# Group 2's first matmul as seven products of half-groups, and token-stationary second matmuls in groups 0 and 1

## The chip, the core and the metric

The kernel runs on one core of a Trainium2 chip. The metric is the device time of one execution in microseconds. A run gives a time; one profiled execution gives a span, which begins at its first instruction, and all durations quoted here. A core has five engines with queues of their own, which run in order and wait for each other only by semaphores: TensorE (PE in the profile, with its weight loads as PEld), VectorE (DVE), ScalarE (ACT), GpSimd (POOL) and SyncE (SP). Data lie in on-chip memory with 128 partitions; matmuls write into eight PSUM banks of 512 floats per partition.

## What is computed

```
w = softmax(weight, axis=-1)                       # [8 heads, 7 taps]
y[b, s, h, :] = sum_k w[h, k] * x_pad[b, s + k, h, :]   # causal window, 24 channels a head
xn = (y - mean(y)) / sqrt(var(y) + 1e-6) * g_ln    # over 192 channels
out = y + relu(xn @ w_ch1) @ w_ch2                 # 192 -> 768 -> 192
```

x is 8 x 4224 x 192 in float32; w_ch1, w_ch2 and g_ln come as float64 and are turned into float32 on the chip. The mean is taken out of w_ch1 in advance ("centring"), and the factor 1/sqrt(var) of a token, `rstd`, is applied to the result of the second matmul, so the first matmul can run on y itself.

## The kernel before

Tokens are worked on in 18 groups. Group 0 has 6 tokens in each of 128 partitions, group 1 has 8 (the rows left over in all batches), group 2 has 10, and groups 3 to 17 have 16. For each group the steps are:

- `first_tap` (ScalarE, L380) writes `y = x * tap 0`, `second_tap` (ScalarE, L398) writes tap 1 into a tile `tb`, and `add_second_tap` (L409) adds `tb` to `y` by an accumulating DMA that GpSimd issues. `conv` (VectorE, L417) adds the other taps, one instruction per tap and head.
- `transpose` (VectorE, L428) makes `yt`, in which a partition block of 32 holds 32 channels. `moments` (VectorE, L448) and `root` (20 small GpSimd operations, L460 to L483) make `rstd`. `store_y` writes y to the output.
- The first matmul: `up` for groups 0 to 2, `up_mixed` for the others. `rows_of_tiles` (L533) is the matmul of both: 32 rows of weights, 128 columns, four at a time, one for each block of 32 partitions.
- The second matmul: `down` (L785) for groups 0 and 1, `down_fast` (L838) from group 2 on; its result is scaled and added to the output by DMA.

`up` runs six passes of 128 hidden columns. Each takes a set of four banks (`take_set`), and ScalarE evicts it with the relu (L523). `take_set` and `take_bank` hand out the eight banks in rotation.

`up_mixed` and `down_fast` replace 8 block products by 7. The operands are cut into quarters, a11 to a22 of y (halves of the tokens by halves of the channels) and b11 to b22 of the weights; sums of the quarters are made beforehand (`sums_of_y`, `w1sums`, `w2sums`; `b12` is replaced by `b12 - b11`). Two bank sets X and Y take the products by turns. A set is read out by ScalarE between products, and some quarters of the result are closed by adding a second product, by an accumulating DMA (`add_by_dma`, L612) or by VectorE (L651). Only after that can ScalarE apply the relu (L658). `lower_sum` and `half_sum` prepare the operands of the second matmul.

`down` of groups 0 and 1 holds 32 columns of w2 as weights and streams the hidden values, so its result is transposed: `park` copies it out of PSUM (ScalarE, L913), `finish` transposes it back (VectorE, L965), and `scale` (ScalarE, L927) applies `rstd`.

The order of the work is written out by hand: instructions run on each engine in the order in which the Python program emits them. The loop over groups at the end emits, for group 0 and 1, what the other engines do during their first matmul and then `down`; `between` puts ScalarE and GpSimd work between the six passes of `up`; `work` is a list of ScalarE pieces that `down_fast` emits behind each of its products, `behind` says how many. `let_in(tile)` is a VectorE write of one element, which makes a later GpSimd write to the tile wait until VectorE has come to that place. Tiles with the same tag share a buffer: y[4] takes the buffer of y[2], and so waits for its store.

The hidden values of all groups lie in one tile, `room` (L184), 12288 floats in each partition. `tb[3]` lies at its end.

Of the kernel before, what the change touches and what calls it, by code (L numbers as in the profile page):

```python
# [16 lines left out]
def kernel(  # L17
# [69 lines left out]
    FC = NF // 2  # L87

# [295 lines left out]
    def second_tap(g, heads=(0, H)):  # L384

        n = groups[g][2]
        if heads[0]:
            pass
        elif g == 2:
            part = upool.tile([P, 3 * HJ * CH * C], F32, tag="ys", name="tb2")  # L390
            tb[g] = part[:, 0 : n * D].rearrange("p (j d) -> p j d", d=D)
        elif g == 3:
            tb[g] = room[:, (NF * NQ * C - D) * J :].rearrange("p (j d) -> p j d", d=D)
        else:
            tb[g] = bpool.tile([P, J, D], F32, tag="tb", name=f"tb{g}")
# [97 lines left out]
    def hidden_tile(g):  # L493
        n = groups[g][2]

        if fast[g]:
            ht[g] = room.rearrange(
                "p (h e f q j t) -> p h e f q j t", h=2, e=2, f=FC, q=NQ, t=width(g)
            )
        else:  # L500
            ht[g] = room[:, 0 : NF * NQ * n * C].rearrange(
                "p (f q j t) -> p f q j t", f=NF, q=NQ, t=C
# [6 lines left out]
    def evict_up(g, f, src):  # L509

        if not fast[g]:
            dst = ht[g][:, f]
# [26 lines left out]
    def between(g, f):  # L539

        if g == 1 and f > 2:
            second_tap(3, heads=[(0, 2), (2, 5), (5, 6)][f - 3])
        elif g == 2:
            if f == 0:
                scale(0, 0, groups[0][2])
                add_to_out(0, 0, groups[0][2])
                nc.gpsimd.memset(xg[4][0:1, 0:PAD, :], 0.0)
            elif f < 3:
                m = groups[1][2]
                scale(1, m * (f - 1) // 2, m * f // 2)  # L550
# [38 lines left out]
    def quarters_of_y(g):  # L589
        if width(g) == C:  # L590
            cuts = [(slice(HJ * h, HJ * h + HJ), slice(0, C)) for h in range(2)]
        else:
            cuts = [(slice(0, J), slice(T * h, T * h + T)) for h in range(2)]
        return [yt[g][:, js, CH * k : CH * k + CH, ts] for js, ts in cuts for k in range(2)]

    def sums_of_y(g, engine):

        room = upool.tile([P, 3 * HJ * CH * C], F32, tag="ys", name=f"ysums{g}")
        room = room.rearrange("p (v j c t) -> p v j c t", v=3, c=CH, t=width(g))
# [11 lines left out]
    def add_by_dma(dst, src):  # L611
        nc.gpsimd.dma_start(out=dst, in_=src, accum_op=ALU.add)  # L612

# [158 lines left out]
    po = {}  # L772

    def down(g):


        n = groups[g][2]
        po[g] = []
        js = slice(0, n)
        w = n * C  # L780
        for c in range(NC):
            bank = take_bank()
            for f in range(NF):
                for q in range(NQ):
                    nc.tensor.matmul(  # L785
                        bank[C * q : C * q + C, 0:w], w2[:, f, C * c : C * c + C], ht[g][:, f, q],
                        start=(f == 0), stop=(f == NF - 1),
                    )
            po[g].append((c, js, bank[:, 0:w]))
# [19 lines left out]
    def lower_sum(g, fs=range(FC)):  # L809

        a = of_products(g)
        if g in MIXED:
# [8 lines left out]
    def down_fast(g, work):  # L821
# [32 lines left out]
        if g == 2:  # L854
            work += [lambda h=h: first_tap(4, heads=(h, h + 1)) for h in range(7, H)]
# [6 lines left out]
        behind = (1, 1, 1, 1) if g == 2 else (3, 2, 2, 3)  # L862
# [42 lines left out]

    def park(g):

        n = groups[g][2]
        pool, room = (cpool, NC * NFAST * C) if g else (bpool, J * D)
        parked = pool.tile([P, room], F32, tag="cs" if g else "tb", name=f"parked{g}")  # L910
        parked = parked[:, 0 : NC * n * C].rearrange("p (c t) -> p c t", c=NC)
        for i, (c, js, src) in enumerate(po[g]):
            nc.scalar.copy(parked[:, c, :], src)  # L913
            po[g][i] = (c, js, parked[:, c, :])
# [38 lines left out]

    def down_rows(g, j):

        rows = take_bank()[:, 0:D]
        for f in range(NF):
            left = rows_left[g][:, f, j - fast[g]]
            nc.tensor.matmul(rows, left, w2[:, f], start=(f == 0), stop=(f == NF - 1))  # L959
        return rows  # L960

    def finish(g):
        ot = out_tile(g)
        for c, js, src in po.pop(g):
            nc.vector.transpose(  # L965
                ot[:, js, C * c : C * c + C], src.rearrange("p (j t) -> p j t", t=C)
            )

# [51 lines left out]
    for g in range(NG):  # L1020
# [59 lines left out]
        if last:  # L1080
# [4 lines left out]
            for j in range(fast[g], groups[g][2]):  # L1085
                add(g, j, down_rows(g, j))
# [34 lines left out]
```

## Time and profile before

| | |
|---|---|
| three runs | 957.99, 958.59 (median), 960.07 us |
| the profiled execution | 958.71 us, span 956.6 us |
| TensorE clock granted | 0.999 |
| TensorE busy | 948.1 us |
| VectorE busy | 891.1 us |
| ScalarE busy | 699.5 us |
| GpSimd busy | 337.9 us |
| first matmul of group 0 / 1 / 2 starts at | 23.05 / 48.85 / 80.28 us |
| second matmul of group 2 starts at | 99.87 us |
| first matmul of group 3 starts at | 117.12 us |

The time is 2.1 us above the span of the same execution. In the lines of the profile, "L417 DVE SCALAR_TENSOR_TENSOR y<-xg,taps,y" is an instruction of kernel line 417 on VectorE that writes y from xg, taps and y; "x40" counts instructions; a line of a timeline begins with the start and the duration in us, and the brackets at its end give the idle time before it and what ended that. Matmuls are pipelined, so their durations overlap, and the pace is read from starts. Each float32 matmul is recorded as two instructions. A line can be that of a helper: L533 is every first matmul, L838 every second matmul by products.

### The profile page before, as it was taken

The numbers are of one execution on the slowest core, as the hardware profiler recorded it, in microseconds if no ns is written. First come the engines' busy times: TensorE is split into PE (matmuls) and PEld (weight loads), VectorE is DVE, ScalarE is ACT, GpSimd is POOL, SyncE is SP. The second block draws the span as 40 slices with busy tenths as digits, with TensorE's granted clock in tenths as the row PEclk, the third lists the DMA queues.
The fourth block names the chain that finished last, engine by engine and source line by source line (L and its number), as shares of the span: only waits on it lengthen the run. The fifth ranks groups of instructions, "written<-read, shape, count | busy, mean of one in ns | idle before, by whom it ended". The sixth has DMA issues, their size and how long they took to land.

```text
span 956.6 us, 38719 instructions
## 1 busy us (share of the span) xinstructions
PE 948.1 (99%) x17266; PEld 725.7 (76%) x17266; DVE 891.1 (93%) x1501; ACT 699.5 (73%) x1174; POOL 337.9 (35%) x472
## 2 busy tenths in 40 slices
PE   8999999999999999999999999999999999999998
PEld 7886886776869687686968778795877869586787
DVE  8989999989999999999999999999999999999757
ACT  7755678586877959687795968779696877967462
POOL 1157522623145142534217141452316332261310
PEclk9999999999999999999999999999999999999999
DMA  8359689589697888979698897969889697778251
GB/s 204 111 153 213 116 224 273 112 178 242 135 258 144 240 162 178 226 136 273 128 250 153 192 221 130 276 131 249 159 194 213 128 275 134 173 136 137 42 96 67
DMA packets 39547, 168.87 MB, mean 177 GB/s; under 512 B 4437, under 2 KB 8150, under 8 KB 33367
## 3 DMA queue, kind: packets, MB, share of 16 engines
q0 software_dynamic: 32576, 106.25, 59.9%
q1 hardware_dynamic: 6800, 60.16, 17.4%
q8 instruction: 135, 2.21, 0.9%
q14 instruction: 30, 0.25, 0.1%
q10 hardware_dynamic: 6, 0.00, 0.0%
HBM read 38.93 MB, written 50.33 MB: 93 GB/s over the span
## 4 chain that ended last, share of the span: by engine, by line
PE 94%; DMA 2%; POOL 1%; DVE 1%; ACT 1%; issue 0%; SPq 0%; ACTq 0%; DVEq 0%; POOLq 0%
PE ps L533 46%; PE ps L838 44%; PE ps L785 3%; DMA xg<-in_x_dram 1%; DVE y L417 1%; PE ps L959 1%; DMA room<-room 1%; DMA out_dram<-y 1%; ACT room L645 0%; ACT y L380 0%; POOL room L612 0%; POOL d L460 0%; POOL r L483 0%; POOL d L479 0%; POOL d L478 0%
## 5 line engine op out<-in xcount | busy, mean ns | idle before, releaser
L417 DVE SCALAR_TENSOR_TENSOR y<-xg,taps,y 128x384 f32<-128x384 f32 (+3 forms) x720 | 361.9, 580 | 3.9 <-DMA y<-tb 2.6
L838 PE MATMUL ps<-room,w2sums 128*32 128x256 f32 (+2 forms) x4608 | 247.4, 371 | 0.0
L533 PE MATMUL ps<-yt,w 32*128 32x256 f32 (+2 forms) x4104 | 235.3, 379 | 2.1 <-DVE yt L428 1.0
L645 ACT COPY room<-ps 128x1024 f32<-128x1024 f32 (+1 forms) x135 | 175.1, 1297 | 79.6 <-PE ps L533 78.6
L533 PEld LDWEIGHTS ps<-yt,w 32*128 32x128 f32 x4104 | 203.7, 185 | 28.9 <-issue 10.1
L838 PEld LDWEIGHTS ps<-room,w2sums 128*32 128x32 f32 x4608 | 149.7, 110 | 91.6 <-ACT room L658 5.3
L838 PE MATMUL ps<-room,w 128*32 128x256 f32 (+2 forms) x3456 | 189.3, 371 | 0.0
L805 DVE TENSOR_TENSOR room<-room 128x1024 f32<-128x1024 f32 (+2 forms) x147 | 161.2, 1171 | 20.8 <-PE ps L838 14.1
L838 PEld LDWEIGHTS ps<-room,w 128*32 128x32 f32 x3456 | 112.3, 110 | 68.9 <-DVE room L651 5.0
L533 PE MATMUL ps<-ysums,w1sums 32*128 32x256 f32 x2160 | 125.2, 379 | 0.0
L533 PEld LDWEIGHTS ps<-ysums,w1sums 32*128 32x128 f32 x2160 | 109.0, 185 | 11.0 <-ACT room L645 3.3
L938 POOL DMA_DIRECT2D out_dram<-ot x69 | 59.3, 989 | 162.1 <-ACT ot L927 105.3
L409 POOL DMA_DIRECT2D y<-tb x59 | 52.5, 1386 | 152.5 <-ACT room L844 110.4
L844 ACT COPY cs<-ps 128x256 f32<-128x256 f32 (+2 forms) x192 | 69.7, 365 | 45.1 <-PE ps L838 45.1
L927 ACT ACTIVATE ot<-ot,r 128x192 f32<-128x192 f32 x232 | 93.9, 462 | 0.0
L658 ACT ACTIVATE room<-room 128x1024 f32<-128x1024 f32 (+1 forms) x89 | 92.7, 1072 | 1.5 <-DMA room<-parts_cs 1.4
L380 ACT ACTIVATE y<-xg,taps 128x384 f32<-128x384 f32 (+3 forms) x141 | 73.2, 608 | 1.2 <-DMA xg<-in_x_dram 0.6
L448 DVE BATCH_NORM_STATS2 st<-y 128x6 f32<-128x192 f32 x264 | 70.1, 346 | 0.0
L844 ACT COPY room<-ps 128x256 f32<-128x256 f32 (+2 forms) x96 | 35.7, 372 | 46.1 <-PE ps L838 44.5
L398 ACT ACTIVATE tb<-xg,taps 128x384 f32<-128x384 f32 (+1 forms) x120 | 66.3, 632 | 0.0
L533 PE MATMUL ps<-yt,w1sums 32*128 32x256 f32 x1080 | 65.4, 381 | 0.4 <-ACT room L645 0.4
L533 PE MATMUL ps<-ysums,w 32*128 32x256 f32 x1080 | 64.5, 376 | 0.0
(113 smaller groups left out, 906.4 us busy)
## 6 DMA issues: line engine op xcount, KB each, us to landing
xg<-in_x_dram SPq DMA_DIRECT2D x14, 2112.0 KB, 16.4
room<-room POOLq DMA_DIRECT2D x45, 512.0 KB, 5.1
out_dram<-ot POOLq DMA_DIRECT2D x59, 384.0 KB, 9.6
y<-tb POOLq DMA_DIRECT2D x58, 384.0 KB, 8.4
out_dram<-y SPq DMA_DIRECT2D x13, 1536.0 KB, 9.5
room<-parts_cs POOLq DMA_DIRECT2D x28, 512.0 KB, 6.9
room<-parts_tb POOLq DMA_DIRECT2D x14, 1024.0 KB, 7.6
xg<-in_x_dram POOLq DMA_DIRECT2D x1, 2112.0 KB, 14.6
```

Source lines behind the costliest of these rows:

```text
L380: nc.scalar.mul(y[g][:, 0:n, cs], xg[g][:, 0:n, cs], taps[:, h, 0:1])
L398: nc.scalar.mul(tb[g][:, 0:n, cs], xg[g][:, 1 : 1 + n, cs], taps[:, h, 1:2])
L417: nc.vector.scalar_tensor_tensor(out=y[g][:, 0:n, cs], in0=t[:, k : k + n, cs], scalar=taps[:, h, k : k + 1], in1=y[g][:, 0:n, cs], op0=AL ...
L448: nc.vector.bn_stats(out=sums[g][:, j, :], in_=y[g][:, j, :])
L533: nc.tensor.matmul(banks[:, q, i * w : i * w + w], right[rows, c, P * i : P * i + P], left[rows, :, c, :], start=(first and c == 0 and i = ...
L645: nc.scalar.activation(dst, src, AF.Relu) if relu else nc.scalar.copy(dst, src)
L658: nc.scalar.activation(c, c, AF.Relu)
L805: nc.vector.tensor_tensor(a[:, *dst, f], a[:, *left, f], a[:, *right, f], op=op)
L838: nc.tensor.matmul(dst[C * q : C * q + C, 0:w], right[:, f, C * c : C * c + C], left[:, f, q], start=(first and f == PAIR), stop=(f == PAI ...
L844: nc.scalar.copy(to[:, c], dst[:, 0:w].rearrange("p (j t) -> p j t", t=t))
L927: nc.scalar.mul(ots[g][:, j, :], ots[g][:, j, :], rstd[g][:, j : j + 1])
L938: nc.gpsimd.dma_start(out=rows[:, d0:d1], in_=src[:, d0:d1], accum_op=ALU.add)
```

## The change

- Group 2's first matmul is made by a new function, `up_whole`: the seven products of `up_mixed` in one pass over all hidden columns, with half-groups of 5 tokens, so each matmul streams 5 x 32 = 160 columns and a set of banks holds 3 x 160 = 480 columns each. The quarter c11 is closed by DMA through a tile of the tag "cs", c22 by DMA through one of the tag "tb", c21 by VectorE. The relus follow.
- `down` of groups 0 and 1 holds 128 tokens of hidden values as weights and streams w2 (192 columns), one row of tokens after another. ScalarE evicts the rows: a copy for group 0, which is scaled later, a multiplication by `rstd` for group 1. `park` and `finish` are gone.
- The sums that group 2's products need are made earlier: the third of `w1sums` in group 0 (by VectorE instead of GpSimd), `b12 - b11`, `sums_of_y(2)` and `moments(2)` in group 1. GpSimd's first three `w2sums` come ahead of the addition of group 3's second tap, behind a `let_in`.
- ScalarE makes group 3's second tap for five heads instead of six; VectorE makes the sixth. The scaling and the output DMAs of groups 0 and 1 and the first taps of group 4 move.

The diff, cut to its core:

```diff
+    FROM_2 = 2 * FC * NQ * J * T - FC * NQ * (J - 6) * C
...
-            tb[g] = room[:, (NF * NQ * C - D) * J :].rearrange("p (j d) -> p j d", d=D)
+            tb[g] = room[:, NF * J * P - n * 5 * GRP :].rearrange("p (j d) -> p j d", d=5 * GRP)
...
     def between(g, f):
         if g == 1 and f > 2:
-            second_tap(3, heads=[(0, 2), (2, 5), (5, 6)][f - 3])
-        elif g == 2:
-            if f == 0:
-                scale(0, 0, groups[0][2])
-                add_to_out(0, 0, groups[0][2])
-                nc.gpsimd.memset(xg[4][0:1, 0:PAD, :], 0.0)
-            elif f < 3:
-                m = groups[1][2]
-                scale(1, m * (f - 1) // 2, m * f // 2)
-                if f == 2:
-                    add_to_out(1, 0, m)
-            else:
-                first_tap(4, heads=[(0, 3), (3, 6), (6, 7)][f - 3])
+            second_tap(3, heads=[(0, 2), (2, 4), (4, 5)][f - 3])
...
+    def up_whole(g):
...
+        X, Y = take_set(), take_set()
...
+        def close(c, banks, pool, tag):
+            part = pool.tile([P, J * D], F32, tag=tag, name=f"parts_{tag}{g}")
+            part = part[:, 0 : FC * NQ * w]
+            nc.scalar.copy(part.rearrange("p (f q w) -> p f q w", f=FC, q=NQ), seen(banks))
+            add_by_dma(c.rearrange("p f q w -> p (f q w)"), part)
...
+        rows_of_tiles(X, a11, b11, True, False, True)
+        nc.scalar.copy(c11, seen(X))
+        rows_of_tiles(Y, a12, b21, True, True, True)
+        close(c11, Y, cpool, "cs")
+        nc.gpsimd.memset(xg[4][0:1, 0:PAD, :], 0.0)
+        rows_of_tiles(X, s2, t[0], False, False, True)
+        nc.scalar.copy(c21, seen(X))
+        rows_of_tiles(Y, s3, t[1], True, False, True)
+        nc.scalar.copy(c22, seen(Y))
+        first_tap(4, heads=(0, 1))
+        rows_of_tiles(X, s1, b12, False, False, True)
+        close(c22, X, bpool, "tb")
+        first_tap(4, heads=(1, 2))
+        rows_of_tiles(Y, a22, t[2], False, True, True)
+        conv(3, 2, 5, heads=(0, 5))
+        conv(3, 5, 6, heads=(0, 3))
+        nc.vector.tensor_tensor(c21, c21, seen(Y), op=ALU.add)
+        rows_of_tiles(X, s4, b22, False, True, True)
+        for f in (PAIR, *range(PAIR)):
+            relu(c11, f)
+        nc.scalar.activation(c12, seen(X), AF.Relu)
+        lower_sum(g, (PAIR, *range(PAIR)))
+        conv(3, 5, 6, heads=(3, 5))
+        conv(3, 6, K, heads=(0, 5))
+        for k in range(2):
+            add_to_out(k, 0, groups[k][2])
+        work = [lambda h=h: first_tap(4, heads=(h, h + 1)) for h in range(2, 5)]
+        work += [lambda f=f: relu(c22, f) for f in (PAIR, *range(PAIR))]
+        return work + [lambda h=h: first_tap(4, heads=(h, h + 1)) for h in range(5, H)]
...
+    def down_row(rows, left):
+        for f in range(NF):
+            nc.tensor.matmul(rows, left(f), w2[:, f], start=(f == 0), stop=(f == NF - 1))
 
     def down(g):
-        for c in range(NC):
-            bank = take_bank()
-            for f in range(NF):
-                for q in range(NQ):
-                    nc.tensor.matmul(
-                        bank[C * q : C * q + C, 0:w], w2[:, f, C * c : C * c + C], ht[g][:, f, q],
-                        start=(f == 0), stop=(f == NF - 1),
-                    )
-            po[g].append((c, js, bank[:, 0:w]))
+        ot = out_tile(g)
+        for j in range(0, groups[g][2], 2):
+            bank = take_bank()[:, 0 : 2 * D].rearrange("p (j d) -> p j d", d=D)
+            for i in range(2):
+                down_row(bank[:, i], lambda f: ht[g][:, f, j + i].rearrange("p q t -> p (q t)"))
+            if g == 0:
+                nc.scalar.copy(ot[:, j : j + 2, :], bank)
+                continue
+            for i in range(j, j + 2):
+                nc.scalar.mul(ot[:, i, :], bank[:, i - j], rstd[g][:, i : i + 1])
...
     def down_fast(g, work):
...
-            work += [lambda h=h: first_tap(4, heads=(h, h + 1)) for h in range(7, H)]
             work += [lambda h=h: second_tap(4, heads=(h, h + 1)) for h in range(H)]
...
-        behind = (1, 1, 1, 1) if g == 2 else (3, 2, 2, 3)
+        behind = (1, 1, 2, 2) if g == 2 else (3, 2, 2, 3)
...
             transpose(g + 1)
-            if g == 2:
-                b11, b12 = quarters_of_w1()[0:2]
-                nc.vector.tensor_tensor(b12, b12, b11, op=ALU.subtract)
...
+        elif g == 2:
+            work = up_whole(g)
         else:
             up(g)
...
             sums_of_quarters(w1sums[:, 0], w11, w1sums[:, 1])
+            nc.vector.tensor_tensor(w1sums[:, 2], w21, w1sums[:, 0], op=ALU.subtract)
             next(root(0, True))
         elif g == 1:
             conv(2, 2)
+            let_in(w2sums[:, 2])
             transpose(2)
             first_tap(3)
-            add_second_tap(3, 6)
+            scale(0, 0, groups[0][2])
             sums_of_quarters(w2sums[:, 2], b12, b22)
             sums_of_quarters(w2sums[:, 0], b12, b11)
             sums_of_quarters(w2sums[:, 1], b22, w2sums[:, 0])
+            add_second_tap(3, 5)
+            sums_of_y(2, nc.gpsimd)
+            moments(2)
+            nc.vector.tensor_tensor(w12, w12, w11, op=ALU.subtract)
             sums_of_quarters(w2sums[:, 3], b21, w2sums[:, 1])
             load_x(4, nc.gpsimd, pad=False)
             store_y(2, nc.gpsimd)
-        elif g == 2:
-            conv(3, 2, 5, heads=(0, 6))
-            lower_sum(2)
-            conv(3, 5, K, heads=(0, 6))
-            let_in(w1sums[:, 2])
-            sums_of_quarters(w1sums[:, 2], w21, w1sums[:, 0])
         if g < 2:
             down(g)
-            park(g)
             if g == 1:
-                moments(2)
-                finish(0)
                 next(root(2, True))
-                conv(3, heads=(6, H))
-                finish(1)
+                conv(3, heads=(5, H))
```

The lower sums of group 2 now apply a relu themselves (the form of L814), and `sums_of_y` and `quarters_of_y` take half-groups of any size.

More of the change, by code (lines that the diff above doesn't have):

```diff
@@ L496, in hidden_tile @@
         if fast[g]:
-            ht[g] = room.rearrange(
+            start = 0 if g in MIXED else FROM_2
+            ht[g] = room[:, start : start + NF * NQ * n * C].rearrange(
                 "p (h e f q j t) -> p h e f q j t", h=2, e=2, f=FC, q=NQ, t=width(g)
@@ L501, in hidden_tile @@
             ht[g] = room[:, 0 : NF * NQ * n * C].rearrange(
-                "p (f q j t) -> p f q j t", f=NF, q=NQ, t=C
+                "p (f j q t) -> p f j q t", f=NF, q=NQ, t=C
             )
@@ L511, in evict_up @@
         if not fast[g]:
-            dst = ht[g][:, f]
+            dst = ht[g][:, f].rearrange("p j q t -> p q j t")
             src = src.rearrange("p q (j t) -> p q j t", t=C)
@@ L590, in quarters_of_y @@
         if width(g) == C:
-            cuts = [(slice(HJ * h, HJ * h + HJ), slice(0, C)) for h in range(2)]
+            n = groups[g][2] // 2
+            cuts = [(slice(n * h, n * h + n), slice(0, C)) for h in range(2)]
         else:
@@ L598, in sums_of_y @@
         room = upool.tile([P, 3 * HJ * CH * C], F32, tag="ys", name=f"ysums{g}")
+        room = room[:, 0 : 3 * groups[g][2] // 2 * CH * C]
         room = room.rearrange("p (v j c t) -> p v j c t", v=3, c=CH, t=width(g))
@@ L612, in add_by_dma, with seen, relu @@
         nc.gpsimd.dma_start(out=dst, in_=src, accum_op=ALU.add)
+    def up_whole(g):
+        n = groups[g][2] // 2
+        w = n * C
+        assert FC * w <= 512
+        hidden_tile(g)
+        a = of_products(g)
+        (c11, c12), (c21, c22) = [
+            [a[:, h, e].rearrange("p f q j t -> p f q (j t)") for e in range(2)] for h in range(2)
+        ]
+        a11, a12, a21, a22 = quarters_of_y(g)
+        s1, s2, s3, s4 = ysums[g]
+        b11, b12, b21, b22 = quarters_of_w1()
+        t = [w1sums[:, k] for k in range(3)]
+        X, Y = take_set(), take_set()
+        def seen(banks):
+            return banks[:, :, 0 : FC * w].rearrange("p q (f w) -> p f q w", w=w)
+        def close(c, banks, pool, tag):
[3 more added lines that the diff above has]
+            add_by_dma(c.rearrange("p f q w -> p (f q w)"), part)
+        def relu(c, f):
+            nc.scalar.activation(c[:, f], c[:, f], AF.Relu)
+        rows_of_tiles(X, a11, b11, True, False, True)
[27 more added lines that the diff above has]
+        return work + [lambda h=h: first_tap(4, heads=(h, h + 1)) for h in range(5, H)]
@@ L770, in up_mixed @@
         return work[0:9] + half + work[9:]
-    po = {}
+    def down_row(rows, left):
+        for f in range(NF):
+            nc.tensor.matmul(rows, left(f), w2[:, f], start=(f == 0), stop=(f == NF - 1))
     def down(g):
[L777 to L780, printed above, removed]
-        for c in range(NC):
-            bank = take_bank()
-            for f in range(NF):
-                for q in range(NQ):
-                    nc.tensor.matmul(
-                        bank[C * q : C * q + C, 0:w], w2[:, f, C * c : C * c + C], ht[g][:, f, q],
-                        start=(f == 0), stop=(f == NF - 1),
-                    )
-            po[g].append((c, js, bank[:, 0:w]))
+        ot = out_tile(g)
[8 more added lines that the diff above has]
+                nc.scalar.mul(ot[:, i, :], bank[:, i - j], rstd[g][:, i : i + 1])
     def quarters_of_w2():
@@ L811, in lower_sum @@
         a = of_products(g)
-        if g in MIXED:
+        if g > 1:
             for f in fs:
@@ L904, in finish_fast @@
             )
[L906 to L914, printed above, removed]
     ots = {}
@@ L952, in store @@
         )
[L954 to L967, printed above, removed]
     idle = take_bank()
@@ L1085 @@
             for j in range(fast[g], groups[g][2]):
-                add(g, j, down_rows(g, j))
+                rows = take_bank()[:, 0:D]
+                down_row(rows, lambda f: rows_left[g][:, f, j - fast[g]])
+                add(g, j, rows)
                 store(g, j, j + 1)
```

## The prediction

> **What bounds the kernel now.** I read the page's busy shares and its chain of waits first, because they tell which engine an edit must touch to move the end.
>
> ```profile
> PE 948.1 (99%) x17266; PEld 725.7 (76%) x17266; DVE 891.1 (93%) x1501; ACT 699.5 (73%) x1174; POOL 337.9 (35%) x472
> PE 94%; DMA 2%; POOL 1%; DVE 1%; ACT 1%; issue 0%; SPq 0%; ACTq 0%; DVEq 0%; POOLq 0%
> ```
>
> TensorE is busy 99% of the span and is 94% of the chain that ended last. Every microsecond that TensorE gains or loses in group 2 therefore reaches the end; nothing later has slack to give it back. Next, TensorE in order of time:
>
> ```profile
> 37.01 11.91 PE L785 MATMUL ps<-room,w 128*32 128x192 f32 x288
> 48.85 15.82 PE L533 MATMUL ps<-yt,w 32*128 32x256 f32 x288
> 64.60 15.75 PE L785 MATMUL ps<-room,w 128*32 128x256 f32 x288
> 80.28 19.66 PE L533 MATMUL ps<-yt,w 32*128 32x320 f32 x288
> ```
>
> These are the second matmul of group 0, both matmuls of group 1 and the first matmul of group 2. The stages touch each other. Four matmuls run side by side and each is two instructions, so eight instructions are a "four": 288 make 36 fours. The first matmul of group 2 costs 19.59 us (80.28 to 99.87), 544 ns a four of 320 columns. Last, GpSimd's order around that stage:
>
> ```profile
> 69.59 3.19 POOL L409 DMA_DIRECT2D y<-room  x2 [10.42 <-ACT y L380]
> 71.50 2.87 POOL L585 TENSOR_TENSOR w2sums<-w 128x288 f32<-128x288 f32 x2
> 74.45 1.69 POOL L585 TENSOR_TENSOR w2sums<-w,w2sums 128x288 f32<-128x288 f32 x2
> 76.08 0.63 POOL L157 DMA_DIRECT2D xg<-in_x_dram  x1
> 76.69 0.56 POOL L489 DMA_DIRECT2D out_dram<-y  x1
> 77.27 0.41 POOL L466 TENSOR_TENSOR d<-st 128x10 f32<-128x10 f32 x1
> ...
> 85.01 0.45 POOL L483 TENSOR_TENSOR r<-r,d 128x10 f32<-128x10 f32 x1
> ```
>
> The second tap of group 3 is added by DMA, then come four subtractions, the load of x for group 4, the store of y for group 2 and the 20 small operations of `root(2)`, to 85.5. Three of these steps are DMAs of one queue.
>
> ```profile
> xg<-in_x_dram POOLq DMA_DIRECT2D x1, 2112.0 KB, 14.6
> y<-room POOLq DMA_DIRECT2D x2, 576.0 KB, 10.2
> out_dram<-y POOLq DMA_DIRECT2D x1, 960.0 KB, 16.3
> ```
>
> From issue to landing (last column): x lands at 76.1 + 14.6 = 90.7 and y at 76.7 + 16.3 = 93.0. The packet records show the queue working one transfer after the other: tap packets of 576 B from 71.8 to 82.3, x from there to about 89, y until 92.
>
> **The change, part by part.** Times are of the profiled execution: span 956.6, time 958.71, near the median of 958.59. I sum against 958.71.
>
> *First matmul of group 2.* Seven products of 3 x 3 x 4 matmuls are 63 fours of 160 columns for 36 of 320. No row shows this line at 160 columns. From below, half of 544 gives 63 x 272 = 17.1 us; the second matmul of the same group at 160 columns ran 63 fours in 17.25 (99.87 to 117.12). From above, the same line at 192 columns took 8.01 us for 24 fours, 334 each: 21.0. I take 17.3, the row of equal width, since at 192 the two lines differ by only 5 ns a four (334 against 329). That is **-2.3** (between -2.5 and +1.4).
>
> *Second matmul of groups 0 and 1.* 36 and 48 token-stationary matmuls of 192 columns, two instructions each. The last group's rows at L959 are exactly this: 48 instructions in 8.07 us, 163 ns from start to start. So 72 x 0.163 = 11.7 (was 11.8) and 96 x 0.163 = 15.6 (was 15.7): **-0.2**. ScalarE evicts the same bytes in fewer or equal pieces, straight to rows; group 0's scaling moves ahead of group 1's evictions (6 x 0.37 = 2.2 us) and delays them, but four banks hold the four row pairs, so TensorE doesn't wait.
>
> *VectorE.* It loses the transposes of `finish` (1.67 + 2.06). It gains the `w1sums` subtraction (1.32, as L873's 128x1152): this stands behind GpSimd's 52.67 and ends near 54.0, in the gap of 2.61 us in which VectorE waited until 54.08 for a DMA, so it costs nothing, or 1.3 without that gap. It gains one more head of the third group's first window tap (0.6), two sums of y (about 0.6 each) and the closing addition of 128x1920 (about 2.2). After the transpose of group 2 (to 71.6) come the sums (1.2), ten statistics (2.65) and `w12 - w11`, moved up from the second matmul (1.3): 77. Eighteen operations on heads 5 to 7 at 0.556 (12 took 6.67) end at 87, eighteen more at 96.5, the closing addition at 98.7. The lower sums wait for the relus of c11, to about 102.3; then 7 operations (3.8), the transpose (3.4) and three half sums (2.2) end at 111.7, and TensorE's fifth product needs them 9.9 us into the second matmul, at 113.2 if that starts at 103.3. Off the path, with 1.5 us to spare.
>
> *A bank that is still being read.* X and Y alternate through seven products, so X has the last one too, and the six banks that the second matmul takes next begin with X's. Its first matmul must wait until ScalarE's relu has read all of X. Before, the last set was the other one and the relu lay beside the products. The cost: 128x1280 took 1.24 and 128x2048 1.87 from PSUM, so 128x1920 is 1.77 by interpolation, with 0.1 at the edges: **+1.9**. It eats most of the gain.
>
> *c11 is closed by DMA.* ScalarE's relu of c11 stands ahead of that relu in its queue, and waits for the DMA that adds the second product. GpSimd now does three subtractions first (gated at 69.5, 0.8 each), so the tap's DMA is issued at 72.0 instead of 69.6; then 3.2 us of issuing, two sums (1.82 for 128x768 gives 1.14 each), the fourth subtraction, x, y, and at 79.5 `root(2)`. Its operations were 0.53 us apart beside the convolution and 0.29 beside the removed transposes: 20 x 0.53 ends at 90. Only then is c11's addition issued. In the queue: tap from 74.2 for about 10, so to 84.2; x lands 8.5 later as before, 92.7; y 2.3 later, 95.0. The 1024 KB additions of the later groups moved their packets in 5.0 us (145.0 to 150.0), so 960 KB take 4.7: c11 lands at **99.7**. With an empty queue it would be 90 + 7.6 (page: parts_tb) = 97.6, from below. Three relus of 128x640 are 1.85 (L658 took 2.00 for two of 1024), to 101.5; the relu of X ends at 103.3 and the second matmul starts there, not at 99.87.
>
> *A wait on ScalarE.* The first tap of group 4 writes the buffer whose store lands at 95.0, and ahead of it the x load must land. It is queued before the copy of X that closes c22, and TensorE's last product waits for that copy: 95.0 + 0.5 + 1.8 = 97.3, product to 99.8, relu of X to 101.7. So this path alone gives a start at 101.7, and is second to c11's.
>
> *ScalarE in the second matmul.* It carries 17 pieces of work where it had 9. Relus of c22 are 0.58 apart; the third product meets the last one about 0.4 late, and a copy 0.1: **+0.5**, between 0 and 1.5.
>
> Sum: 103.3 - 99.87 = +3.4, which holds -2.3, -0.2, +1.9 and a further 4.0 of waiting, plus 0.5 in the second matmul, less about 0.6 because I take the middle of c11's landing between 97.6 and 99.7 rather than its late end: **+3.3, 962.0 us**.
>
> [...] The tap's runs were 576 B, 2048 of them in 10.4 us; they become 480 B. By bytes they take 8.7, by packets 10.4; I took 10. [...] No run here shows a 480 B addition. [...]
>
> **Rivals.**
>
> *The queue is not late: no change.* TensorE alone would end the last product at 80.1 + 17.3 = 97.4. If c11 lands by 95.6 (1.85 earlier) and the store by 92.6, only the bank wait and the ScalarE lag stay: -2.3 - 0.2 + 1.9 + 0.5 = -0.1, 958.6. For it: x's packets start when the tap is done, and 8.7 us by bytes brings everything 1.3 earlier. Against it: GpSimd's issue near 90 plus 7.6. The deciding point is c11's landing: each microsecond past 95.6 is one of TensorE, so it is "no change" up to about 97.6.
>
> *The bank wait doesn't happen: faster.* Were the relu of X hidden and c11 early, -2.5 stay: 956.2. Against it: the rotation of eight banks leaves no other set.
>
> *Shorter matmuls are not cheaper.* If weight loads set the pace, 334 ns a four make the stage 21.0 us, and the change doesn't do what it says. The loads take 185 ns at any width here, yet the 192-column stage stays within 5 ns of the other line. The last product would end near 101.5, just at c11's relus, so the time becomes about 962 to 963: hardly told apart by time, but by the trace.
>
> [...]
>
> **How the numbers follow.** Forecast (962.0, own range 960.6 to 965, with the weight-load rival in it) 0.56; no change 0.28; faster 0.07; jam 0.09. A measurement of this kernel can tell about 0.2%, 1.9 us, from no change. Faster is the bank rival: 0.07. Same: 0.28. Slower: forecast and jam, 0.65. The range runs from 957.5, below the no-change case, to 966, and leaves out the faster case and most of the jam.
>
> **What would show it.** In the profile after: 504 matmuls of 32x160 in L533; a TensorE gap of 2 to 5 us before the second matmul of group 2, ended by ScalarE's relu of X; ScalarE waiting for a DMA on `room` before the relus of c11, landing between 97 and 100; the tap DMA issued near 72 and `root(2)` ending near 90; ScalarE's first tap of group 4 waiting near 94. No gap over 2 us there makes the forecast wrong; a gap elsewhere makes my reasons wrong.

## The result, and the profile after

The changed kernel takes 970.13 us (median of 4 runs, 968.87 to 971.80) against 958.36: a ratio of 1.0123, 95% interval 1.0111 to 1.0135. It is 1.2% slower. I had forecast 962.0 and a range up to 966. The profiled execution took 969.76 with a span of 967.7, 11.1 us more than that of the kernel before.

The page of the changed kernel, first its busy times and then the shares of its last chain: TensorE's busy time hardly moved (948.1 before). What grew is the time in which it stands still, from 8.5 us of the span to 19.1. The 81% is no sign of that: this chain reaches back only to 150.33 us, to VectorE's work ahead of the gap in group 3, where its shares add up to 84% of the span:

```profile
PE 948.6 (98%) x17074; PEld 741.1 (77%) x17074; DVE 894.8 (92%) x1495; ACT 703.7 (73%) x1170; POOL 343.0 (35%) x475
PE 81%; POOL 1%; DMA 1%; DVE 1%; ACT 0%; issue 0%; ACTq 0%; POOLq 0%
```

Next is TensorE of the changed kernel in order of time, as before (start, duration, what, count, idle time before and what ended it):

```profile
80.84 5.17 PE L535 MATMUL ps<-yt,w 32*128 32x160 f32 x144
85.83 2.74 PE L535 MATMUL ps<-ysums,w1sums 32*128 32x160 f32 x73
90.38 2.59 PE L535 MATMUL ps<-ysums,w1sums 32*128 32x160 f32 x68 [1.81 <-issue]
...
100.00 1.37 PE L535 MATMUL ps<-yt,w 32*128 32x160 f32 x32 [0.65 <-issue]
103.25 2.65 PE L889 MATMUL ps<-room,w 128*32 128x160 f32 x72 [1.89 <-ACT room L655]
105.72 0.99 PE L889 MATMUL ps<-room,w2sums 128*32 128x160 f32 x23
108.19 2.61 PE L889 MATMUL ps<-room,w2sums 128*32 128x160 f32 x65 [1.48 <-issue]
111.15 2.11 PE L889 MATMUL ps<-room,w2sums 128*32 128x160 f32 x56 [0.34 <-ACT room L633]
...
113.99 2.50 PE L889 MATMUL ps<-room,w 128*32 128x160 f32 x65 [0.47 <-issue]
```

For comparison, three rows of the kernel before: the start of group 2's second matmul, the one gap without a releaser in group 3, and the start of group 3's second matmul.

```profile
99.87 2.65 PE L838 MATMUL ps<-room,w 128*32 128x160 f32 x72
120.22 0.91 PE L533 MATMUL ps<-yt,w 32*128 32x256 f32 x9 [0.66 <-issue]
146.13 4.09 PE L838 MATMUL ps<-room,w 128*32 128x256 f32 x72
```

The products run at the pace I took (144 instructions, 18 fours, in 4.99 us: 277 ns a four), and the wait for the bank before 103.25 is there, 1.89 us. But four gaps have no releaser ("issue"), 4.4 us in all, in the middle of products whose operands were long ready. Later, in group 3, stands the longest gap (the same view of a later stretch), and behind it a slower clock (the second fence, two windows of the changed kernel: length, busy time and count of TensorE, its weight loads, VectorE, ScalarE and GpSimd, then the granted clock, DMA share and GB/s):

```profile
155.83 5.78 PE L889 MATMUL ps<-room,w 128*32 128x256 f32 x72 [4.10 <-DVE room L702]
```

```profile
156.00:185.00 29.00, 29.00 (x508) 16.98 (x504) 26.27 (x38) 19.26 (x45) 8.61 (x9) 0.94 0.84 218
156.74:160.15 3.41, 3.41 (x40) 1.74 (x36) 3.41 (x6) 2.02 (x4) 0.00 (x1) 0.50 0.00 0
```

The 0.94 is one stretch of 3.41 us at half clock, from 156.74 on, and full clock for the rest: 72 instructions that took 4.09 us before take 5.78, 1.7 us more. The landmarks give the balance against the kernel before: group 2's first matmul starts 0.56 later, its second 3.38, group 3's first 6.63, its second 9.70, group 4's first 10.70. From there to the end only 0.3 is added. The first 0.56 is no price of the change: in the 14 profiles of this case that stage starts anywhere from 79.6 to 81.7 us.

**The gaps without a releaser** are late instructions. The changed kernel's page has a DMA queue of the kind "instruction":

```profile
q8 instruction: 134, 2.20, 0.9%
```

These are 134 packets of 16,384 B. TensorE ran 34,148 matmuls and weight loads and 169 instructions of its sequencer, 34,317 in all: one packet for 256 instructions, a block. I counted the instructions that TensorE had started when it stopped (the table has the start of the last of them). A stop comes at 449 + 256k, k being the blocks delivered ahead of the one in the third column, and ends 0.9 to 1.4 us after that one has arrived:

```
last start   instructions started   next block arrives   TensorE resumes
88.28        2241 = 449 +  7*256    89.48                90.38
99.06        2753 = 449 +  9*256    98.67                99.99
106.42       3009 = 449 + 10*256    106.83               108.19
113.22       3265 = 449 + 11*256    112.55               113.99
```

The one gap of this kind in group 3 of the kernel before (0.66 at 119.6) stands at 4289 = 449 + 15 x 256. No packet starts before TensorE has started 154 + 256k instructions, so I take that as the call; this is inferred, the trace shows no call. From the call to the packet's start the kernel before needed 0.7 us (median) where the DMA engines were under 0.6 busy, and 4.2 where they were over 0.9; the changed kernel 0.7 and 3.8. Between call and stop lie 295 instructions, matmuls and weight loads: about 5 us at 160 columns (17 ns an instruction), 8 at 256, 10 at 320, by the pace of each. Short matmuls and full DMA engines together are what fails.

**The gap in group 3** begins on ScalarE, GpSimd and the DMA queue. In order of time, GpSimd's DMA issues in the changed kernel, in the second fence VectorE, and in the third the issue of group 4's second tap in the kernel before:

```profile
72.10 3.19 POOL L410 DMA_DIRECT2D y<-room  x2
...
90.88 0.90 POOL L604 DMA_DIRECT2D room<-parts_cs  x1
...
118.23 3.58 POOL L410 DMA_DIRECT2D y<-tb  x4 [7.99 <-ACT room L895]
```

```profile
129.09 1.30 DVE L949 STREAM_TRANSPOSE ot<-cs 128x320 f32<-128x320 f32 x3
135.95 14.90 DVE L418 SCALAR_TENSOR_TENSOR y<-xg,taps,y 128x384 f32<-128x384 f32 x28 [5.56 <-DMA y<-tb]
```

```profile
108.59 3.57 POOL L409 DMA_DIRECT2D y<-tb  x4 [3.37 <-ACT tb L398]
```

Group 4's second tap is issued at 118.23 (before: 108.59), because it stands behind ScalarE's 17 pieces, in a matmul that started 3.4 us later and lost 2 us to late blocks; it is still moving when x of group 5 starts at 127, and VectorE waits for it until 135.95. VectorE's closing addition of group 3 (L702) then ends 4 us after TensorE needs its bank.

### The profile page after: what moved, and what is told of

Read it like the earlier page. It is cut to its first block, busy times and chain, and to the rows that moved or that the text cites. A ratio compares the mean times of both kernels' runs of the same rounds, so it can differ in the third digit from the quotient of the medians.

```text
span 967.7 us, 38332 instructions
## 1 busy us (share of the span) xinstructions
PE 948.6 (98%) x17074; PEld 741.1 (77%) x17074; DVE 894.8 (92%) x1495; ACT 703.7 (73%) x1170; POOL 343.0 (35%) x475
## 4 chain that ended last, share of the span: by engine, by line
PE 81%; POOL 1%; DMA 1%; DVE 1%; ACT 0%; issue 0%; ACTq 0%; POOLq 0%
PE ps L889 42%; PE ps L535 38%; PE ps L826 1%; DMA room<-room 1%; ACT room L696 0%; DVE room L702 0%; DVE y L418 0%; POOL room L604 0%; POOL d L461 0%; POOL d L479 0%; POOL r L484 0%; POOL d L480 0%; DVE room L865 0%; DVE y L979 0%; POOL d L467 0%
## 5 line engine op out<-in xcount | busy, mean ns | idle before, releaser
L535 PE MATMUL ps<-yt,w 32*128 32x256 f32 (+2 forms) x4032 | 223.4, 370 | 2.5 <-ACT room L525 1.1
L535 PEld LDWEIGHTS ps<-yt,w 32*128 32x128 f32 x4032 | 197.1, 185 | 24.0 <-issue 9.5
L889 PE MATMUL ps<-room,w 128*32 128x256 f32 (+2 forms) x3456 | 191.8, 374 | 6.5 <-DVE room L702 4.1
L856 DVE TENSOR_TENSOR room<-room 128x1024 f32<-128x1024 f32 (+2 forms) x144 | 158.9, 1178 | 25.8 <-PE ps L889 19.2
L535 PE MATMUL ps<-ysums,w1sums 32*128 32x256 f32 (+1 forms) x2304 | 130.5, 374 | 1.8 <-issue 1.8
L535 PEld LDWEIGHTS ps<-ysums,w1sums 32*128 32x128 f32 x2304 | 114.2, 185 | 12.9 <-issue 4.8
L964 ACT ACTIVATE ot<-ot,r 128x192 f32<-128x192 f32 x224 | 90.9, 464 | 0.0
L535 PE MATMUL ps<-yt,w1sums 32*128 32x256 f32 (+1 forms) x1152 | 68.0, 375 | 0.3 <-ACT room L696 0.2
L535 PE MATMUL ps<-ysums,w 32*128 32x256 f32 (+1 forms) x1152 | 67.3, 371 | 0.0
```

The lines of the kernel that those rows point to most:

```text
L535: nc.tensor.matmul(banks[:, q, i * w : i * w + w], right[rows, c, P * i : P * i + P], left[rows, :, c, :], start=(first and c == 0 and i = ...
L856: nc.vector.tensor_tensor(a[:, *dst, f], a[:, *left, f], a[:, *right, f], op=op)
L889: nc.tensor.matmul(dst[C * q : C * q + C, 0:w], right[:, f, C * c : C * c + C], left[:, f, q], start=(first and f == PAIR), stop=(f == PAI ...
L964: nc.scalar.mul(ots[g][:, j, :], ots[g][:, j, :], rstd[g][:, j : j + 1])
```

## The experiments

Medians, and ratios to the kernel before timed on the same chip, with 95% intervals. "The changed kernel" is 970.13.

**The bank.**

```diff
+        if g == 2:
+            turn[0] += 4
         banks = [take_bank() for c in range(CH) for i in range(2)]
```

> The changed kernel, with the bank rotation moved on by one set ahead of group 2's second matmul, so that its six banks begin with Y's and not with X's, which hold the last product. Theory (the second matmul waits 1.9 us for the relu that reads X): the 1.89 us gap ahead of it shrinks to 0.3 or less, and since nothing else holds its start, the time falls by 1.5 to 1.9 us, to about 968.4. Rival (c11's relus, which wait for the DMA until 99.0, hold the start anyway): the gap stays over 1 us, now put down to a relu of c11, and the time falls by less than 0.6.

969.49, 1.0123 (1.0106 to 1.0140): nothing gained. TensorE of this kernel in order of time:

```profile
101.60 2.98 PE L891 MATMUL ps<-room,w 128*32 128x160 f32 x72
104.40 0.99 PE L891 MATMUL ps<-room,w2sums 128*32 128x160 f32 x23
108.50 2.61 PE L891 MATMUL ps<-room,w2sums 128*32 128x160 f32 x65 [3.11 <-issue]
```

Both theories were wrong. The wait of 1.89 is gone and the second matmul starts 1.65 us earlier, but TensorE stops at the same 23rd instruction of the second product until the same time, 108.5 for 108.2: the gap grew from 1.48 to 3.11. The block had been called for well before the bank wait in both (98.4 and 98.7) and arrived at 106.8 and 107.1. From the start of the first matmul to that of the second 1.9 us are gained, and 1.4 of them go to the block. Behind the gap in group 3 (3.97 us) the clock is then at half for 6.8 us, where the changed kernel had 3.4, and that takes another 1.2.

**Group 4's second tap.**

```diff
-            work += [lambda h=h: second_tap(4, heads=(h, h + 1)) for h in range(H)]
+            pass
```

> The changed kernel without group 4's second window tap: ScalarE doesn't make it and no DMA adds it, so group 4's result lacks that tap. Theory (the late landing of this DMA at 135.95 makes VectorE wait 5.56 us, so group 3's closing addition is late, TensorE waits 4.10 us for it, and its clock then falls to 0.94): the gap ahead of group 3's second matmul goes, the clock stays at 1.00, and the time falls by 4 to 5.5 us, to about 965. Rival (VectorE is late by its own work, which is 6 us behind the kernel before): the gap keeps over 2 us and the time falls by less than 2.

962.93 (961.05 to 965.81), 1.0055 (1.0034 to 1.0076): 7.2 us less, more than expected. TensorE of this kernel at group 3's second matmul:

```profile
152.71 4.09 PE L889 MATMUL ps<-room,w 128*32 128x256 f32 x72
```

It starts right behind the first, and its 72 instructions take 4.09 us again. The theory of the late tap holds: in the profiled run the two matmuls of group 3 take 55.3 us for 61.1, 5.8 less. The rest is within what the runs of this kernel differ by (4.8 us).

**The token-stationary second matmuls alone,** on the kernel before.

```diff
-            park(g)
...
-                finish(0)
...
-                finish(1)
```

together with the new `down` and the row layout of `ht`.

> The kernel before with one part of the change alone: token-stationary second matmuls in groups 0 and 1, without the parking, the transposes back and group 1's separate scaling; group 2's first matmul stays in six passes. Theory (these matmuls cost TensorE the same, and VectorE is not on the path there): within 0.6 us of the kernel before, with the two stages at 11.9 and 15.8 us as in the changed kernel. Rival (the VectorE time that is freed, 3.7 us, itself brings something): faster by 1 us or more. Rival (part of the change's loss sits here): slower by 1 us or more.

957.82, 0.9996 (0.9986 to 1.0006): no difference. This part costs nothing, and the VectorE time that it frees brings nothing by itself.

**Less DMA traffic.**

```diff
-            store_y(2, nc.gpsimd)
...
-        for k in range(2):
-            add_to_out(k, 0, groups[k][2])
```

> The changed kernel without the store of group 2's y and without the adding of groups 0 and 1's results to the output, so those rows are wrong; 2.1 MB less goes through the DMA queue between 89 and 113 us. Theory (TensorE's gaps without a releaser, 1.81, 0.65, 1.48 and 0.47 us between 88 and 114, are instruction blocks of 16 KB fetched too late because the DMA engines are full): at least those after 97 us go, and the time falls by 3 to 4.5 us. Rival (they come from the rate of instructions alone, 17 ns each at 160 columns): the gaps stay, 3 us or more in sum, and the time falls only by what an earlier c11 gives, under 1 us.

966.48, 1.0086 (1.0071 to 1.0101): 3.7 us less, as the theory had it. TensorE of this kernel, its gaps only:

```profile
89.51 2.59 PE L535 MATMUL ps<-ysums,w1sums 32*128 32x160 f32 x68 [0.55 <-issue]
99.95 1.37 PE L535 MATMUL ps<-yt,w 32*128 32x160 f32 x32 [1.46 <-issue]
153.16 4.09 PE L887 MATMUL ps<-room,w 128*32 128x256 f32 x72 [3.78 <-DVE room L700]
```

The gaps at 106.4 and 113.2 are gone and the first shrank to 0.55. But, against my expectation, not all after 97 us went: the one before the last product grew to 1.46, while c11's and c22's additions still move. The gap in group 3 stayed, 3.78, but here no slower clock follows it: the 72 instructions take 4.09 us.

**More DMA traffic in the kernel before,** in a stage of equally short matmuls.

```diff
+                for k in (NG - 2, NG - 1):
+                    bb, j0, m = groups[k]
+                    nc.sync.dma_start(
+                        out=outr[bb, :, j0 * D : (j0 + m) * D],
+                        in_=y[3].rearrange("p j d -> p (j d)"),
+                    )
```

> The kernel before, unchanged in its matmuls, with two more stores of 1.5 MB (of group 3's y, into rows that are written again later) from SyncE at about 102.5 us, in the middle of group 2's second matmul, whose matmuls are as short (160 columns) as those of the change. Theory (traffic delays instruction blocks, and at 17 ns an instruction the block in store runs out after some 5 us): the delay of the blocks called for at 104.5, 108.9 and 113.2 us rises from 0.8 us to 3 to 6, TensorE shows one or two gaps without a releaser of 0.5 to 2 us each between 104 and 120, and the time rises by 0.5 to 4 us. Rival (the gaps of the changed kernel come from its own instruction stream): no such gap beyond the 0.66 at 119.6 that is there already, and no change over 0.5.

964.17, 1.0062 (1.0049 to 1.0075): 6.2 us more, beyond what I expected. TensorE of this kernel in order of time, and then a window with columns as above:

```profile
111.48 4.55 PE L838 MATMUL ps<-room,w2sums 128*32 128x160 f32 x127 [1.58 <-DVE room L805]
118.52 1.07 PE L838 MATMUL ps<-room,w2sums 128*32 128x160 f32 x17 [2.48 <-issue]
```

```profile
118.00:124.00 6.00, 5.49 (x101) 5.12 (x104) 5.86 (x18) 1.17 (x4) 2.33 (x2) 0.72 1.03 361
```

The gaps stand at 3777 = 449 + 13 x 256 and 4033 = 449 + 14 x 256 instructions. The view puts the first down to VectorE, but VectorE's operation had ended at 109.6: it was the block, which arrived at 110.09. The blocks called for at 104.6 and 108.9 needed 4.6 and 7.3 us to their packet's start, for 0.8 in the kernel before. So the gaps need nothing of the change. They make 4.7 us from start to start; another 1.7 is the clock, 0.72 on average behind the second gap, which is 3.4 us at half.

**The load of x for group 5, later.**

```diff
             sums_of_y(g + 1, nc.gpsimd)
-            if g == 2:
-                load_x(5, gate=True)
             moments(g + 1)
+            if g == 2:
+                load_x(5, gate=True)
```

> The changed kernel with one move: the load of x for group 5 is let in behind group 3's statistics, about 4 us later, instead of ahead of them. Theory (group 4's second tap, added by DMA from 119.7 us on, lands only at 135.95 because from 127 it shares the DMA engines with this load): it lands near 129 to 130, VectorE's wait of 5.56 us falls below 1, the 4.10 us gap ahead of group 3's second matmul and the clock of 0.94 behind it go, and the time falls by 4 to 5.5 us, to about 965. Rival (the tap is late because ScalarE makes it late, at 117.8, and lands 14 us later whatever stands beside it): VectorE waits over 4 us still, and the time stays within 1.

965.81, 1.0081 (1.0058 to 1.0104), but its four runs are 963.0, 963.3, 968.4 and 968.7. The profiled one is 968.68: the 4.10 us gap is gone (group 3's second matmul starts at 151.56, 27.96 after the first), and two stops at 449 + 256k, 1.15 and 2.92 us, have come at 157 and 165. The theory holds for the gap; the moved traffic meets other blocks. The times stand in two pairs 5 us apart, so those stops may come in some runs and not in others; one profile doesn't settle it.

**The store of group 2's y on SyncE's queue.**

```diff
-            store_y(2, nc.gpsimd)
+            store_y(2)
```

> The changed kernel with the store of group 2's y on SyncE's queue: it moves its 1 MB near 71 us, when the DMA engines are idle, and not behind x of group 4 between 88 and 94. Theory (full DMA engines delay TensorE's instruction blocks, and c11's addition stands behind the store): c11 lands near 97.5 instead of 99.0, the gap of 1.81 us near 88 keeps 0.5 or more because x of group 4 still moves then, the 0.65 near 99 goes or shrinks; the second matmul of group 2 starts 0.6 to 2 us earlier and the time falls by 0.5 to 2 us, or by more if the second tap is then no longer caught by the load of x. Rival (the gaps don't depend on the traffic): gaps of 1.81 and 0.65 as before and a change below 0.5.

969.17, 1.0118 (1.0105 to 1.0131): at most 1 us. The gap near 88 fell from 2.10 to 1.00 between starts, the next rose from 0.94 to 1.48, the one at 106.4 went; the second matmul starts 0.9 earlier and group 3's second 1.5. The clock eats it: it is at half for 3.4 us from 102.2 and for 6.8 from 153.4, behind the gap of 3.79 in group 3, where the changed kernel had 3.4 in all.

**Four mends together,** the two moves above, the rotation, and `root(2)` behind c11's addition.

```diff
+        next(root(2, True))
         first_tap(4, heads=(0, 1))
...
+        if g == 2:
+            turn[0] += 4
...
+            moments(g + 1)
             if g == 2:
                 load_x(5, gate=True)
-            moments(g + 1)
...
-            store_y(2, nc.gpsimd)
+            store_y(2)
...
-                next(root(2, True))
```

> The changed kernel with four mends together: bank rotation moved on by one set ahead of group 2's second matmul, the store of group 2's y on SyncE's queue, the load of x for group 5 behind group 3's statistics, and root(2) behind the addition of c11 on GpSimd. Theory (the loss is bank wait, late instruction blocks and the late tap, on top of a true gain of 2.3 us in the products): 960 to 963 us, level with the kernel before or up to 0.5% slower, since some blocks are still late; below 958 only if the gaps without a releaser fall under 1 us in sum. Rival (the loss lies in something these four don't touch, such as ScalarE's extra work): above 965.

968.50, 1.0129 (1.0095 to 1.0163), with runs from 963.9 to 975.7: the 960 to 963 that I expected are missed, and the spread leaves the time inconclusive. In the profiled run (963.89) the tap's gap is gone, stops of 1.56 and 2.96 us stand at 449 + 256k in the products, and one of the mends costs time itself: `root(2)` now stands ahead of c22's addition on GpSimd, and TensorE waits 2.20 us at 110.85 for c22's first relu.

**Everything blamed taken away.** In the changed kernel (e9_clean), and but for the bank's rotation in the kernel before too (e10_clean_before, there by its own lines for the same additions, tap and transfers):

```diff
-        for k in range(2):
-            add_to_out(k, 0, groups[k][2])
...
+        if g == 2:
+            turn[0] += 4
...
-            work += [lambda h=h: second_tap(4, heads=(h, h + 1)) for h in range(H)]
+            pass
...
-            load_x(4, nc.gpsimd, pad=False)
-            store_y(2, nc.gpsimd)
+            load_x(4, pad=False)
```

> The changed kernel with everything taken away that the runs so far blame: bank rotation moved on by one set, no second tap of group 4, no store of group 2's y, no adding of groups 0 and 1's results to the output (these parts of the result are wrong), and x of group 4 loaded on SyncE's queue near 70 us. Theory (63 short fours for 36 long ones are worth 2.1 us, and bank, blocks and tap cost the rest): gaps without a releaser under 0.7 us in sum between 80 and 120, second matmul of group 2 at 98.3 to 99.5, time 1 to 2.5 us below its partner from the kernel before. Rival (something else of the change costs time too): level with its partner or slower.

> The partner: the kernel before with the same things left out (no second tap of group 4, no store of group 2's y, no adding of groups 0 and 1's results, x of group 4 on SyncE's queue). Theory (none of them is on the kernel's path): within 0.8 us of the kernel before, and at most the 0.66 us gap at 119.6 goes. Rival (they cost the kernel before time as well): faster by over 1.5 us.

958.12, 1.0003 (0.9993 to 1.0013), and 957.73, 0.9991 (0.9982 to 0.9999). The partner lost nothing that counts. The changed kernel comes down by 12 us to level with it, and not below as I had expected: in group 2 one stop is left (e9_clean, TensorE in order of time),

```profile
97.92 2.12 PE L535 MATMUL ps<-yt,w 32*128 32x160 f32 x32 [1.94 <-issue]
```

with the clock at 0.89 from 90 to 105, half of full from 98.39 to 101.80. It falls while c11's and c22's own additions move, and nothing else does. In the profiled runs the stop and the clock take more than the 2.1 us of gain: from the start of group 2's first matmul to that of group 3's, 39.2 us for the partner's 36.8. Behind that the two take the same within 0.2 us, so nothing later costs time; e9_clean's profile only began that stage 1.7 us earlier.

**The whole change in another order,** nothing left out (as the expectation lists it).

```diff
+            store_y(2)
+            load_x(4, pad=False)
...
+        first_tap(4, heads=(0, 4))
         rows_of_tiles(X, a11, b11, True, False, True)
...
-        behind = (1, 1, 2, 2) if g == 2 else (3, 2, 2, 3)
+        behind = (0, 1, 2, 2) if g == 2 else (3, 2, 2, 3)
```

> The whole change, nothing left out, in another order: rotation moved on by one set; store of group 2's y and load of x for group 4 on SyncE's queue near 70 us; groups 0 and 1 added to the output before c11 and not after c22; root(2) behind c22's addition; all first taps of group 4 inside the seven products, so that behind them ScalarE has 11 pieces and not 17 and the second tap is issued near 109 instead of 118. Theory: second matmul of group 2 at 98.5 to 101, second tap landed by 121, no wait for group 3's closing addition, blocks still late by 0 to 2 us while the DMA engines are full until 102: 957 to 960.5 us, level with the kernel before. Rival (late blocks take whatever is freed): over 962.

961.34, 1.0039 (1.0024 to 1.0055): 3.2 us over its own kernel before are left of 11.8, a little more than the 957 to 960.5 that I expected. No wait in group 3; one late block of 2.83 us before the last product, where c11 and c22 are added (TensorE in order of time):

```profile
100.59 1.37 PE L535 MATMUL ps<-yt,w 32*128 32x160 f32 x32 [2.83 <-issue]
```

**And c11 closed by VectorE.**

```diff
-        close(c11, Y, cpool, "cs")
+        nc.vector.tensor_tensor(c11, c11, seen(Y), op=ALU.add)
```

> The reordered kernel of the run before (e11_order) with one more change: c11 is closed by VectorE, right after the second product, and not by DMA; the window taps of group 3 on VectorE are split so that this comes at its time. It takes 1 MB of additions out of 92 to 97 us and costs VectorE 2.1 us. Theory (the block that is called for near 93 us is late because of c11's and c22's own additions, which made the 2.8 us gap near 97 in e11_order): this gap falls below 1 us, the second matmul of group 2 starts at 98.6 to 100.5, and the time falls by 1 to 3 us against e11_order, to 958.5 to 960.5. Rival (c22's addition alone is enough to delay the block, or VectorE's 2.1 us are now on the path ahead of the half sums): the gap stays or a wait for VectorE of 1 to 2 us takes its place, and the time stays within 1 us of e11_order's 961.3.

964.59, 1.0073 (1.0059 to 1.0087): slower than the run before, by the rival's second half, and by more than the rival said. TensorE of this kernel in order of time:

```profile
98.83 2.98 PE L893 MATMUL ps<-room,w 128*32 128x160 f32 x72
...
114.80 6.77 PE L893 MATMUL ps<-room,w2sums 128*32 128x160 f32 x144 [3.48 <-DVE room L858]
```

All late blocks of group 2 are gone, so c11's addition was what delayed the one of 2.83, and the first matmul of group 2 at last takes 18.6 us (80.26 to 98.83) for 19.6: 1.0 of the 2.1 that the pace promises. But VectorE's half sums are now 3.5 us late, and the clock falls behind that gap (6.77 us for 5.07). VectorE has no 2 us to give in this order; an order with the half sums ahead of some window taps was not tried. No version beat the kernel before.

## Why the prediction was wrong

It was wrong in size: slower, as forecast, but over three times as much (11.8 us for 3.3). By its steps:

- *Products:* -2.3 forecast; at 277 ns a four 17.5 us, so -2.1. Right as work. **This is the step that failed first:** the row of equal width that I took the price from, 17.25 us, was measured where the DMA engines were 0.17 busy (104 to 111 us) when it called for its blocks at 104.5 and 108.9. Their share was 1.08 only from 111 on, and the block that was late there stopped TensorE in group 3, the 0.66 at 119.6. The same instructions under a load of 0.87 to 0.99 (90 to 109 us of the changed kernel) wait for their blocks: 4.4 us with group 2's second matmul. I had looked at data, banks and queues, and put nothing down for TensorE's own instructions.
- *Second matmuls of groups 0 and 1:* -0.2 forecast; the stages are 11.90 and 15.80, +0.1 each. Alone they change nothing (e3_down).
- *VectorE:* hidden, as said; `w12 - w11` took 1.88 for 1.3.
- *Bank:* +1.9; measured 1.89. But e1_banks shows that it can't be added to the rest: without it TensorE waits 1.6 us longer for the next block.
- *c11 and the queue:* tap issued at 72.10 (72.0), c11 at 90.88 (90), its relus from 99.0 (99.7), second matmul at 103.25 (103.3). The last number is right for another reason: the late blocks put the end of the last product at 101.4, and c11 was ready by then. The tap's packets took 7.8 us (74.27 to 82.10), not 10.
- *ScalarE in the second matmul:* +0.5 forecast between 0 and 1.5. TensorE's wait for the relus is 0.34. **This is the second step that failed:** I priced the 17 pieces by what TensorE waits for in that stage, and not by what stands behind them on GpSimd. The second tap of group 4 moved by 9.6 us, more than the 3.4 by which TensorE was late, met the next load, and cost 4.1 us and then 1.7 of clock in group 3.
- *"Nothing later has slack":* right here (10.7 us behind at group 4, 11.0 at the end), and true of VectorE too. Its closing addition of group 3 ended at 146.04 in the kernel before, and TensorE started on it at 146.13.
- *Rivals:* the jam (chance 0.09, a time from 965 up) had the size, and nothing else came true. It was my estimate for a tap at half the rate or a GpSimd held longer; no run shows the first, the tap took 7.8 us, GpSimd issued c11's addition at 90.88 for 90, and VectorE worked from 77.66 to 98.20 without a wait for the tap.
- *Its own signs:* the gap before the second matmul is 1.89 us, under the 2 that the forecast asked for, and most of the loss stands elsewhere, which was to mean that the reasons are wrong.

By the landmarks, the 11 us are: 0.6 ahead of group 2; 2.8 in its first matmul (2.5 of late blocks and 1.9 of bank, less 2.1 of products, and 0.5 of edges, since each stop takes 0.3 more from start to start than its idle time); 3.3 in its second (2.0 of late blocks, 0.3 for the relus, the rest edges); 3.1 in group 3's first (4.1 for the tap, less the late block that the kernel before had there, 1.0 from start to start); 1.0 in group 3's second (1.7 of clock, less 0.7 that the kernel before lost there for reasons I didn't look into); and 0.3 behind it. What calls a block, and which packets it stands behind, the trace doesn't show; and I leave it open. The spread of e5_x5_later and e7_all probably comes from there and from the clock; one profile of each doesn't show it.

## What to carry to other kernels

Before replacing long matmuls by more and shorter ones, multiply: the instructions between call and stop by the time of each, against the delay of an instruction block where the DMA engines are full (here 295 x 17 ns = 5 us against some 4 us to the packet's start, 1 for the packet and 1.4 until TensorE resumes). A price taken from a quiet stretch didn't hold in a full one (17.25 us for 63 fours that called for their blocks at a DMA share of 0.17; 4.4 us of stops in group 2 of the changed kernel at 0.87 to 0.99). And a piece of work that is moved on one engine is priced by the last thing queued behind it on the others (here 4.1 us in group 3), not by the next wait that it causes (0.34).

## What the runs showed of the hardware

- TensorE stopped when it had started 449 instructions and 256 more for each block that had been delivered, in 30 stops of over 0.6 us from start to start in the 14 kernels here, and resumed 0.9 to 1.6 us after the next 16 KB block had arrived. In the changed kernel q8 moved 134 such packets for 34,317 instructions of TensorE, one for 256. The packet itself takes 0.9 to 1.9 us. No packet started while more than 295 instructions were left before the stop (the changed kernel; 281 in the kernel before), a little over one block, and a stop cost up to 3.11 us of idle time (e1_banks).
- Gaps of TensorE can cost again through the clock: 1.7 us behind the 4.10 of the changed kernel. In the clock records of the 14 profiles it is 1.00 or 0.50 and changes only in steps of 3.41 us, and how long a gap is doesn't decide alone. Behind 4.10 us in the changed kernel it was 0.50 for 3.41 us, behind 3.97 (e1_banks) and 3.79 (e6_sp_store) for 6.83, behind 2.48 (e8_more_dma) and 1.94 (e9_clean) for 3.41, and behind 3.78 (e4_quiet) and 2.83 (e11_order) not at all. What differs is where the gap lies in the steps. In the changed kernel the 4.10 fall into a step with 1.6, followed by full clock, and one with 2.5, followed by half; in e4_quiet the 3.78 fall into two steps, 2.0 and 1.8 us, both followed by full clock. In the 14 profiles, from 20 us on, the steps at full clock that were followed by half had 1.85 to 3.1 us of idle time, and none with more than 2.0 was followed by full clock. So whether a gap cost again here was in part luck.
- Additions by DMA in runs of 480 B (the changed kernel's second tap of group 3) moved about 290 packets in a microsecond, those of 576 B (the kernel before) about 200: 0.14 MB against 0.12. The length of the runs isn't all of it: with the next load of x on another queue it was 360 to 370 (e9_clean) against 210 to 315 (e10_clean_before).
